# Re-timing the first 46 steps, the exponential's table, the fold blocks and the last group of a fused attention and feed-forward kernel

## The chip, the cores and the metric

The kernel runs on one core of one Trainium2 chip. The metric is the device time in microseconds (us) of one execution. PE is the tensor engine, PEld its weight loads, DVE is VectorE, ACT is ScalarE, POOL is GpSimd and SP is SyncE.

## The reference

Cross-covariance attention on 4 batches of 6080 rows and 256 columns is followed by a feed-forward block on all 24320 rows. The result is float32.

```python
def _attn_ref(q, k, v, tau):
    qn = q / (np.linalg.norm(q, axis=1, keepdims=True) + 1e-06)
    kn = k / (np.linalg.norm(k, axis=1, keepdims=True) + 1e-06)
    s = kn.transpose(0, 2, 1) @ qn / tau
    s = s - s.max(-1, keepdims=True)
    a = np.exp(s)
    a /= a.sum(-1, keepdims=True) + 1e-09
    return (v @ a).astype(np.float32)          # (4, 6080, 256)

def _moe_ref(x, w_in, w_out, s, b):            # x: (24320, 256)
    h = x @ w_in                               # 256 -> 2048
    r = np.maximum(h, 0.0)
    g = s * (r * r) + b
    return (g @ w_out).astype(np.float32)      # 2048 -> 256
```

## The kernel before

The attention matrix of a batch is only 256 x 256, so the kernel never forms `v @ a`. It multiplies the attention matrix into `w_in` ("folds" it) and gets a weight `wa` for each batch. The rows are cut into 48 groups of 512 (the last is shorter), and each group takes 16 steps. A step makes one 128-wide block of h with two 128x512 matmuls. ACT takes the relu of two steps at a time, and the squares are shared between ACT and DVE.

The second matmul of groups 1 to 46 is a scheme of seven products in place of eight. It needs sums S1 to S4 of blocks of g, which DVE makes for each group, and combinations T1, T2, T3 and N4 of blocks of `w_out`, which are made once, early in the program. Groups 0 and 47 use a plain second matmul ("slots" of four 128x256 matmuls). Meanwhile the q and k rows of the next batch arrive in chunks, and PE accumulates their product for the next attention matrix ("gram").

In these traces PE keeps the order in which the loop below emits its instructions, even where it has to stand: in the changed kernel a gram matmul waits 2.00 us for its load, and the h block that is emitted behind it starts only after it, at 76.09 us, though the last relu before it had ended at 74.94. So that order is the schedule. `at_step` puts a piece of side work at the end of a step.

```python
qk_pool = pool("qk_pool", 6)       # q/k chunks, and at first the four pieces of w_out
...
def exps():                        # Gram.finish_ops
    st["e"] = sm_pool.tile([P, CH, C], FP16, tag="eT", name="eT")
    for j in range(CH):
        po(nc.scalar.activation(out=st["e"][:, j, :], in_=st["t"][:, j, :], func=AF.Exp,
                                scale=st["r"][:, 0, j : j + 1]))
...
def fold_both(f0, n):              # first two blocks of w_in, for group 0
    def f():
        wa_ps = h_tile("wa_ps")    # one PSUM tile, read by ACT (m = 0) and DVE (m = 1)
        for m in range(CH):
            fold_mm(f0, n, m, wa_ps[:, m, :n])
        for m in range(CH):
            scaled(f0, n, m, wa_ps[:, m, :n])
    return f
...
w_pieces = []                      # w_out, 4 pieces of 512 KB
for i in range(NPIECE):
    w32 = qk_pool.tile([P, 4, C], FP32, tag="qk", name="w32")
    ...
for i, f in enumerate(fin[9:]):                        # the other fold blocks
    at_step(max(0, i // 2 * 4 - 1) + i % 2, f)
for i in range(NPIECE):
    at_step(6 + i, lambda i=i: cast_w_out(i))          # DVE: fp16 copy for groups 0 and 47
for i in range(NPIECE + 1):
    at_step(10 + i, lambda i=i: rowconst_sum(i))       # DVE: row sums of w_out
at_step(21, rowconst_mm)
for i in range(NPIECE):
    at_step(14 + 2 * i, lambda i=i: combine_w(i))      # DVE: 4 combinations
    at_step(22 + 3 * i, lambda i=i: cast_w(i))         # ACT: T2 and T3, last readers of a piece
...
for b in range(1, B):                                  # q/k chunks of the next batch
    w0 = first_group[b - 1] * FT + (26 if b == 1 else 6)
    for c in range(NCH):
        sc = w0 + span * c * JC / n
        at_step(max(3, sc - 16), lambda gr=gr, c=c: gr.load(c))
        ...
PLAG = {0: 11, NG - 1: 5}
SQUARES = {3: (0, 1, nc.scalar), 5: (1, 2, nc.scalar), 8: (2, 4, nc.vector),
           12: (4, 6, nc.vector)}
SUMS = {2: 1, 3: 2, 6: 3, 10: 4}
for s in range(NS + FT):
    g, m = divmod(s, FT)
    if g < NG:
        mm1(g, m)
    ...                                                # products of the group before
    for gp in plain:
        mp = s - PLAG[gp] - gp * FT
        if 0 <= mp < FT:
            plain_mm2(gp, mp)
    if g < NG and m % 2 == 1:
        relu(g, m // 2)
    ...
    if m == 0 and 0 < g and g - 1 not in plain:
        square(g - 1, 6, 8, nc.vector)
    if 0 < g and g - 1 not in plain and m in SUMS:
        sums_of(g - 1, SUMS[m])
    for f in side.pop(s, []):
        f()
```

## Time and profile before

| kernel | median us | range us | runs |
|---|---|---|---|
| before | 732.67 | 732.56 to 733.0 | 3 |

The busy shares of the page (engine, busy us, share of the span, instructions):

```profile
PE 706.2 (97%) x7618; PEld 510.1 (70%) x7618; DVE 626.5 (86%) x877; ACT 537.5 (74%) x574; POOL 82.3 (11%) x158
```

PE has 24.6 us without work in 730.8, and 14.2 of these lie before 38 us, in the load of the first batch. The list of PE's waits tells whose they are (total us, times, longest). The prediction shows four of its lines; these are the two largest (three more, of 0.5 us or less, are left out):

```profile
PE s_ps L142 <- ACT qk L133: 9.0, 2, 7.1
PE s_ps L142 <- DMA qk<-in_q_dram: 4.6, 6, 1.1
```

Both belong to the load of the first batch, before 38 us. In the timeline (start us, duration us, engine, line, operation, count, and in brackets the idle time just before and what ended it) two places matter. The first is the matmul that reads the first sum of group 1, the second the first gram matmul of chunk 2 of batch 1, at step 40. Neither waits:

```profile
72.90 0.44 PE L683 MATMUL o_ps<-T,S 128*128 128x128 f16 x5
...
76.03 0.38 PE L142 MATMUL s_ps<-qk 128*128 128x256 f16 x2
```

### The profile page before, as it was taken

To read this page: it belongs to the slowest core of one execution; us is meant where nothing else is said; L and a number is where in the kernel's file an instruction comes from. 1 tells how busy PE (TensorE), PEld (TensorE's weight loads), DVE (VectorE), ACT (ScalarE), POOL (GpSimd) and SP (SyncE) were. 2 spreads that over 40 slices of the span, in tenths; PEclk is the share of its full clock that TensorE was granted. 3 is DMA by queue.
4 is the path that set the end of the run, shared out by engine and by line. 5 is a ranking of instruction groups with operands and counts; after the bars stand their busy time and mean duration, and the time that the engine had idled before them with its cause. 6 is when DMAs were issued, how large, how long until landed. Compare 5 with 4: busy or idle time off the path is not lost.

```text
span 730.8 us, 17839 instructions
## 1 busy us (share of the span) xinstructions
PE 706.2 (97%) x7618; PEld 510.1 (70%) x7618; DVE 626.5 (86%) x877; ACT 537.5 (74%) x574; POOL 82.3 (11%) x158
## 2 busy tenths in 40 slices
PE   4788999999999999999999999999999999999997
PEld 3555777776677777776677777777668777777776
DVE  4779999988889989988788989998888888888886
ACT  4468877788777777887777778777877777777772
POOL 4523110001111110001010210000000000000000
PEclk9999999999999999999999999999999999999999
DMA  9999995235487764333666685332333333321201
GB/s 236 209 250 134 205 165 96 58 92 123 92 146 161 121 99 95 91 70 73 131 125 137 121 147 126 70 66 66 83 73 78 87 74 73 97 57 60 65 30 74
DMA packets 81600, 79.57 MB, mean 109 GB/s; under 512 B 55696, under 2 KB 56528, under 8 KB 81520
## 3 DMA queue, kind: packets, MB, share of 16 engines
q0 software_dynamic: 21472, 39.46, 31.8%
q1 hardware_dynamic: 59616, 37.64, 19.9%
q8 instruction: 60, 0.98, 0.6%
q10 hardware_dynamic: 432, 1.31, 0.5%
q14 instruction: 20, 0.16, 0.1%
HBM read 78.91 MB, written 24.90 MB: 142 GB/s over the span
## 4 chain that ended last, share of the span: by engine, by line
PE 85%; ACT 6%; DVE 4%; DMA 4%; issue 1%; POOL 0%; ACTq 0%; POOLq 0%; DVEq 0%
PE h_ps L541 41%; PE o_ps L683 37%; PE s_ps L142 4%; ACT r L551 3%; DMA qk<-in_q_dram 2%; PE wa_ps L274 2%; DMA raw<-in_q_dram 1%; ACT g L562 1%; DVE g L564 1%; PE o_ps L589 1%; ACT L247 1%; ACT sq L165 1%; DVE acc L427 0%; ACT L222 0%; DVE w_out L448 0%
## 5 line engine op out<-in xcount | busy, mean ns | idle before, releaser
L551 ACT ACTIVATE r<-h_ps 128x1024 f16<-128x1024 f32 (+1 forms) x384 | 388.6, 1015 | 162.0 <-PE h_ps L541 158.6
L541 PE MATMUL h_ps<-vT,wa 128*128 128x512 f16 (+7 forms) x1632 | 452.5, 364 | 4.4 <-ACT r L551 3.1
L683 PEld LDWEIGHTS <-S 128*128 128x128 f16 x2944 | 198.1, 98 | 86.6 <-issue 1.3
L683 PEld LDWEIGHTS <-g 128*128 128x128 f16 x2208 | 155.0, 98 | 74.1
L564 DVE TENSOR_TENSOR g<-r 128x2048 f16<-128x2048 f16 (+2 forms) x154 | 176.7, 1148 | 21.7 <-ACT r L551 21.4
L683 PE MATMUL o_ps<-T,S 128*128 128x128 f16 x2208 | 183.6, 219 | 1.1 <-DVE S L609 0.7
L541 PEld LDWEIGHTS <-wa 128*128 128x128 f16 x1632 | 136.5, 98 | 25.7 <-issue 4.8
L683 PE MATMUL o_ps<-w_out,g 128*128 128x128 f16 x1472 | 134.2, 219 | 0.0
L569 DVE SCALAR_TENSOR_TENSOR o_sb<-o_ps,s_out,u 128x256 f32<-128x256 f32 x138 | 66.3, 480 | 51.6 <-PE o_ps L683 49.6
L562 ACT ACTIVATE g<-r 128x1024 f16<-128x1024 f16 x92 | 97.0, 1054 | 0.0
L320 POOL DMA_DIRECT2D v<-in_v_dram x48 | 25.7, 535 | 514.7 <-DMA vT<-v 334.1
L142 PE MATMUL s_ps<-qk 128*128 128x256 f16 (+1 forms) x384 | 70.5, 285 | 13.6 <-ACT qk L133 9.0
L569 DVE SCALAR_TENSOR_TENSOR u<-o_ps,s_out,rowconst 128x256 f32<-128x256 f32 x138 | 65.9, 478 | 2.4 <-PE o_ps L683 2.4
L683 PE MATMUL o_ps<-N,g 128*128 128x128 f16 x736 | 63.5, 219 | 0.0
L683 PE MATMUL o_ps<-w_out,S 128*128 128x128 f16 x736 | 63.4, 219 | 0.0
L165 ACT ACTIVATE sq<-qk 128x1024 f16<-128x1024 f16 (+3 forms) x49 | 50.4, 1033 | 10.1 <-DMA qk<-in_k_dram 4.9
L611 DVE TENSOR_TENSOR S<-S,g 128x2048 f16<-128x2048 f16 x46 | 56.3, 1224 | 1.3
L609 DVE TENSOR_TENSOR S<-g 128x2048 f16<-128x2048 f16 x46 | 55.9, 1214 | 0.0
L615 DVE TENSOR_TENSOR S<-g,S 128x2048 f16<-128x2048 f16 x46 | 55.9, 1214 | 0.0
L613 DVE TENSOR_TENSOR S<-g 128x2048 f16<-128x2048 f16 x46 | 55.8, 1214 | 0.0
L142 PEld LDWEIGHTS <-qk 128*128 128x128 f16 (+1 forms) x384 | 33.2, 102 | 19.6 <-DVE qk L132 8.3
L162 DVE TENSOR_TENSOR sq<-qk 128x1024 f16<-128x1024 f16 (+3 forms) x49 | 33.0, 673 | 2.2 <-DMA qk<-in_q_dram 2.2
(67 smaller groups left out, 280.9 us busy)
## 6 DMA issues: line engine op xcount, KB each, us to landing
out_dram<-o_sb SPq DMA_DIRECT2D x46, 512.0 KB, 3.0
v<-in_v_dram POOLq DMA_DIRECT2D x47, 256.0 KB, 3.8
qk<-in_k_dram POOLq DMA_DIRECT2D x42, 256.0 KB, 6.6
qk<-in_q_dram POOLq DMA_DIRECT2D x42, 256.0 KB, 7.6
vT<-v SPq DMA_TRANSPOSE x182, 2.8
w<-in_moe_w_out_dram POOLq DMA_DIRECT2D x4, 512.0 KB, 11.3
raw<-in_q_dram ACTq DMA_DIRECT2D x2, 512.0 KB, 6.9
raw<-in_k_dram SPq DMA_DIRECT2D x2, 512.0 KB, 6.7
```

Of the source, the lines that this page charges most:

```text
L142: po(nc.tensor.matmul(self.s_ps[:, ch, :], kc[:np_, j, ts(ch, P)], qc[:np_, j, :], start=(c == 0 and j == 0 and ch == 0), stop=(c == len(s ...
L165: po(nc.scalar.activation(out=st["sq"][:np_, 1, js, :], in_=kc[:np_, js, :], func=AF.Square))
L541: po(nc.tensor.matmul(dst, wa[:, ci, ts(m, P)], src, start=(ci == 0), stop=(ci == CH - 1), skip_group_check=True))
L551: po(nc.scalar.activation(out=r16[:, :, i % 2, :n], in_=h_tiles.pop((g, i))[:, :, :n], func=AF.Relu))
L562: po(nc.scalar.activation(out=dst, in_=src, func=AF.Square))
L564: po(nc.vector.tensor_mul(dst, src, src))
L569: po(nc.vector.scalar_tensor_tensor(out=dst, in0=src, scalar=s_out, op0=ALU.mult, in1=add, op1=ALU.add))
L609: po(nc.vector.tensor_add(S[1], A21, A22))
L611: po(nc.vector.tensor_sub(S[2], S[1], A11))
L613: po(nc.vector.tensor_sub(S[3], A11, A21))
L615: po(nc.vector.tensor_sub(S[4], A12, S[2]))
L683: po(nc.tensor.matmul(st[name][:, j, :], a()[:, i, ts(j, P)], w[:, i, :], start=first, stop=last, skip_group_check=True))
```

## The change

Its intent is to keep PE fed where it waits for ACT and DVE. It has five parts.

1. The 16 output slots of group 0 go to steps 11 to 33 instead of 11 to 26, so that the steps after 26 aren't h matmuls alone.
2. The preparation of `w_out` (casts, row sums, combinations, T casts) is spread out to follow the arrival of its pieces. Three casts move from DVE to ACT, and the combinations are ordered so that neighbours don't depend on each other.
3. The exponential's table is loaded by a small activation a few steps ahead (`ready`), and the two exponentials stand in different steps.
4. The two first fold blocks write a PSUM tile for each reader, the factor 1/LAM moves into the summed column, and both folds of the second block come at step 0.
5. In the last group, the first two sums are done in halves and one square goes to ACT.

```diff
+            def ready():
+                po(nc.scalar.activation(out=warm, in_=ones32[:, 0:1], func=AF.Exp))
-            def exps():
-                ... both exponentials ...
+            def exps(j):
+                ... one exponential ...
...
-                                            ones16[:, 0:1], start=(ch == 0 and j == 0),
+                                            parts16, start=(ch == 0 and j == 0),
-                po(nc.vector.tensor_scalar_mul(out=st["rs"], in0=r_ps, scalar1=1.0 / LAM))
-                po(nc.vector.reciprocal(out=st["rs"], in_=st["rs"]))
+                po(nc.vector.reciprocal(out=st["rs"], in_=r_ps))
...
-                    wa_ps = h_tile("wa_ps")
+                    two = [self.bank("wa_ps", CH, C)[:, 0, :n], h_tile("wa_ps")[:, 0, :n]]
...
+    FIN = (0, 3, 3, 6, 8, 10, 13)
-        at_step(max(0, i // 2 * 4 - 1) + i % 2, f)
+        at_step(i // 2 * 4 - 1 + i % 2 if i > 1 else 0, f)
+    RC = (13, 16, 19, 21, 23)      # row sums
+    CO = (7, 14, 18, 24)           # casts of w_out: the first on DVE, the others on ACT
+    CW = (17, 20, 25, 27)          # combinations, for two pieces at a time
+    CT = (32, 34, 36, 38)          # T2 casts; T3 casts six steps later
-        at_step(6 + i, lambda i=i: cast_w_out(i))
+        at_step(CO[i], lambda i=i: cast_w_out(i))
-        at_step(10 + i, lambda i=i: rowconst_sum(i))
-    at_step(21, rowconst_mm)
+        at_step(RC[i], lambda i=i: rowconst_sum(i))
+    at_step(30, rowconst_mm)
-        at_step(14 + 2 * i, lambda i=i: combine_w(i))
-        at_step(22 + 3 * i, lambda i=i: cast_w(i))
+        at_step(CW[i], lambda i=i: combine_w(i // 2, i % 2))
+        at_step(CT[i], lambda i=i: cast_w(T2, i))
+        at_step(CT[i] + 6, lambda i=i: cast_w(T3, i))
-                at_step(8, lambda g=g: transpose_v(g))     # group 1
+                at_step(12, lambda g=g: transpose_v(g))
...
+    LAST = {0: last_squares, 2: lambda: sums_of(NG - 2, 1, NP // 2, NP),
+            3: lambda: sums_of(NG - 2, 2, 0, NP // 2), 5: lambda: sums_of(NG - 2, 2, NP // 2, NP)}
-            mp = s - PLAG[gp] - gp * FT
-            if 0 <= mp < FT:
-                plain_mm2(gp, mp)
+            for mp in range(FT):
+                if s == gp * FT + PLAG[gp] + (mp * 3 // 2 if gp == 0 else mp):
+                    plain_mm2(gp, mp)
```

More of the change, by code (lines that the diff above doesn't have):

```diff
@@ L242, in turn @@
                             st["t"][:, j, ts(ch, P)], st["s"][:, ch, ts(j, P)], ident32))
-            def exps():
-                st["e"] = sm_pool.tile([P, CH, C], FP16, tag="eT", name="eT")
-                for j in range(CH):
-                    po(nc.scalar.activation(
-                        out=st["e"][:, j, :], in_=st["t"][:, j, :], func=AF.Exp,
-                        scale=st["r"][:, 0, j : j + 1]))
-                self.wa = apool.tile([P, CH, Dff], FP16, tag="wa16", name="wa16")
+            def ready():
+                po(nc.scalar.activation(out=warm, in_=ones32[:, 0:1], func=AF.Exp))
+            def exps(j):
+                if j == 0:
+                    st["e"] = sm_pool.tile([P, CH, C], FP16, tag="eT", name="eT")
+                po(nc.scalar.activation(
+                    out=st["e"][:, j, :], in_=st["t"][:, j, :], func=AF.Exp,
+                    scale=st["r"][:, 0, j : j + 1]))
+                if j == 0:
+                    self.wa = apool.tile([P, CH, Dff], FP16, tag="wa16", name="wa16")
             def sums():
@@ L279, in f @@
                 def f():
-                    wa_ps = h_tile("wa_ps")
+                    two = [self.bank("wa_ps", CH, C)[:, 0, :n], h_tile("wa_ps")[:, 0, :n]]
                     for m in range(CH):
-                        fold_mm(f0, n, m, wa_ps[:, m, :n])
+                        fold_mm(f0, n, m, two[m])
                     for m in range(CH):
-                        scaled(f0, n, m, wa_ps[:, m, :n])
+                        scaled(f0, n, m, two[m])
                 return f
@@ L301, in finish_ops @@
                       for m in range(CH)]
-            return [norms, recip, turn, exps, sums] + folds
+            return [norms, recip, ready, turn, lambda: exps(0), lambda: exps(1), sums] + folds
         def bank(self, name, a, b):
@@ L351 @@
     nc.vector.memset(ones16, 1.0)
+    parts16 = consts.tile([P, 1], FP16)
+    nc.vector.memset(parts16, 1.0 / LAM)
     ones32 = consts.tile([P, P], FP32)
@@ L415 @@
     fin[1]()
+    fin[2]()
     keep_busy(5, w_in16[:, 0, :P], w_in16[:, 0, :NW])
-    fin[2]()
+    fin[3]()
     transpose_v(0)
-    for f in fin[3:9]:
+    for f in fin[4:11]:
         f()
@@ L435, in rowconst_mm, with combine_w, cast_w_out, cast_w @@
         po(nc.vector.tensor_scalar_mul(out=rowconst, in0=rc_ps, scalar1=b_bc))
-    def combine_w(i):
-        w = w_pieces[i].rearrange("p (i h) c -> p h i c", h=2)
-        B11, B12 = w[:, 0, :, :P], w[:, 0, :, P:]
-        B21, B22 = w[:, 1, :, :P], w[:, 1, :, P:]
-        part = ts(i, 2)
-        po(nc.vector.tensor_sub(T1[:, part, :], B12, B11))
-        po(nc.vector.tensor_sub(B12, B22, B12))
-        po(nc.vector.tensor_add(B11, B11, B12))
-        po(nc.vector.tensor_sub(N4[:, part, :], B21, B11))
-    def cast_w_out(i):
-        po(nc.vector.tensor_copy(out=w_out16[:, ts(i, 4), :], in_=w_pieces[i]))
-    def cast_w(i):
-        w = w_pieces[i].rearrange("p (i h) c -> p h i c", h=2)
-        po(nc.scalar.copy(out=T2[:, ts(i, 2), :], in_=w[:, 0, :, :P]))
-        po(nc.scalar.copy(out=T3[:, ts(i, 2), :], in_=w[:, 0, :, P:]))
+    def combine_w(i, k):
+        for n in (2 * k, 2 * k + 1):
+            for p in (2 * i, 2 * i + 1):
+                w = w_pieces[p].rearrange("p (i h) c -> p h i c", h=2)
+                B11, B12 = w[:, 0, :, :P], w[:, 0, :, P:]
+                B21, B22 = w[:, 1, :, :P], w[:, 1, :, P:]
+                part = ts(p, 2)
+                if n == 0:
+                    po(nc.vector.tensor_sub(T1[:, part, :], B12, B11))
+                elif n == 1:
+                    po(nc.vector.tensor_sub(B12, B22, B12))
+                elif n == 2:
+                    po(nc.vector.tensor_add(B11, B11, B12))
+                else:
+                    po(nc.vector.tensor_sub(N4[:, part, :], B21, B11))
+    def cast_w_out(i):
+        if i == 0:
+            po(nc.vector.tensor_copy(out=w_out16[:, ts(i, 4), :], in_=w_pieces[i]))
+        else:
+            po(nc.scalar.copy(out=w_out16[:, ts(i, 4), :], in_=w_pieces[i]))
+    def cast_w(T, i):
+        w = w_pieces[i].rearrange("p (i h) c -> p h i c", h=2)
+        po(nc.scalar.copy(out=T[:, ts(i, 2), :], in_=w[:, 0, :, :P] if T is T2 else w[:, 0, :, P:]))
     side = {}
@@ L459, in at_step @@
         side.setdefault(int(s), []).append(f)
+    FIN = (0, 3, 3, 6, 8, 10, 13)
     first_group = [b * N // TG for b in range(B)]
-    for i, f in enumerate(fin[9:]):
-        at_step(max(0, i // 2 * 4 - 1) + i % 2, f)
+    for i, f in enumerate(fin[11:]):
+        at_step(i // 2 * 4 - 1 + i % 2 if i > 1 else 0, f)
     at_step(14, lambda: po(nc.vector.tensor_scalar_mul(
         out=s_out, in0=s_bc, scalar1=1.0 / (LAM * LAM))))
+    RC = (13, 16, 19, 21, 23)
+    CO = (7, 14, 18, 24)
+    CW = (17, 20, 25, 27)
+    CT = (32, 34, 36, 38)
     for i in range(NPIECE):
-        at_step(6 + i, lambda i=i: cast_w_out(i))
+        at_step(CO[i], lambda i=i: cast_w_out(i))
     for i in range(NPIECE + 1):
-        at_step(10 + i, lambda i=i: rowconst_sum(i))
-    at_step(21, rowconst_mm)
+        at_step(RC[i], lambda i=i: rowconst_sum(i))
+    at_step(30, rowconst_mm)
     for i in range(NPIECE):
-        at_step(14 + 2 * i, lambda i=i: combine_w(i))
-        at_step(22 + 3 * i, lambda i=i: cast_w(i))
+        at_step(CW[i], lambda i=i: combine_w(i // 2, i % 2))
+        at_step(CT[i], lambda i=i: cast_w(T2, i))
+        at_step(CT[i] + 6, lambda i=i: cast_w(T3, i))
     for g in range(NG):
@@ L506, in fin_step @@
             for i, f in enumerate(ops):
-                at_step(int(s) + 1 + ((0, 3, 6, 9, 13)[i] if i < 5 else 16 + (i - 5) * 3), f)
+                at_step(int(s) + 1 + (FIN[i] if i < 7 else FIN[6] + 3 + (i - 7) * 3), f)
         at_step(w1 - fin_len, fin_step)
@@ L601, with sums_of @@
     S = {}
-    def sums_of(g, n):
-        G = g_tiles[g]
+    def sums_of(g, n, i0=0, i1=NP):
+        G = g_tiles[g][:, :, i0:i1]
         A11, A12 = G[:, 0, :, : TG // 2], G[:, 1, :, : TG // 2]
         A21, A22 = G[:, 0, :, TG // 2 :], G[:, 1, :, TG // 2 :]
-        S[n] = spool.tile([P, NP, TG // 2], FP16, tag=f"S{n}", name=f"S{n}")
+        if i0 == 0:
+            S[n] = spool.tile([P, NP, TG // 2], FP16, tag=f"S{n}", name=f"S{n}")
+        T = {k: t[:, i0:i1] for k, t in S.items()}
         if n == 1:
-            po(nc.vector.tensor_add(S[1], A21, A22))
+            po(nc.vector.tensor_add(T[1], A21, A22))
         elif n == 2:
-            po(nc.vector.tensor_sub(S[2], S[1], A11))
+            po(nc.vector.tensor_sub(T[2], T[1], A11))
         elif n == 3:
-            po(nc.vector.tensor_sub(S[3], A11, A21))
+            po(nc.vector.tensor_sub(T[3], A11, A21))
         else:
-            po(nc.vector.tensor_sub(S[4], A12, S[2]))
+            po(nc.vector.tensor_sub(T[4], A12, T[2]))
     def seven_items(g):
@@ L697, with last_squares @@
     SUMS = {2: 1, 3: 2, 6: 3, 10: 4}
+    def last_squares():
+        sums_of(NG - 2, 1, 0, NP // 2)
+        square(NG - 2, 7, 8, nc.scalar)
+        square(NG - 2, 6, 7, nc.vector)
+    LAST = {0: last_squares, 2: lambda: sums_of(NG - 2, 1, NP // 2, NP),
+            3: lambda: sums_of(NG - 2, 2, 0, NP // 2), 5: lambda: sums_of(NG - 2, 2, NP // 2, NP)}
     for s in range(NS + FT):
@@ L722 @@
             square(g, *SQUARES[m])
-        if m == 0 and 0 < g and g - 1 not in plain:
+        if g == NG - 1 and m in LAST:
+            LAST[m]()
+        elif m == 0 and 0 < g and g - 1 not in plain:
             square(g - 1, 6, 8, nc.vector)
-        if 0 < g and g - 1 not in plain and m in SUMS:
+        elif 0 < g and g - 1 not in plain and m in SUMS:
             sums_of(g - 1, SUMS[m])
```

## The prediction

> **What bounds the kernel now.** I read four views in this order: the page's busy shares, a table of stretches, the list of what the tensor engine (PE) waited for, and the timeline at each of those waits. The busy shares say 706.2 of 730.8 us for PE, with VectorE (DVE) at 86% and ScalarE (ACT) at 74%. The table of stretches (PE, PEld, DVE, ACT, POOL busy, then clock, DMA share, GB/s) shows where the missing 25 us lie.
>
> ```profile
> 0.00:10.00 10.00, 1.87 (x8) 1.12 (x8) 1.51 (x4) 2.76 (x4) 5.41 (x16) 1.00 0.87 259
> 50.00:60.00 10.00, 10.00 (x70) 6.76 (x69) 9.86 (x18) 5.28 (x6) 0.07 (x1) 1.00 1.21 167
> 60.00:70.00 10.00, 8.17 (x49) 4.62 (x48) 9.01 (x18) 9.67 (x16) 4.16 (x8) 1.00 0.80 132
> 200.00:650.00 450.00, 448.63 (x4978) 327.29 (x4976) 392.84 (x532) 342.29 (x358) 39.23 (x74) 1.00 0.48 99
> 710.00:720.00 10.00, 9.31 (x130) 8.37 (x128) 8.78 (x15) 4.01 (x6) 0.00 (x0) 1.00 0.14 54
> ```
>
> Most of the idle time is the load of the first batch, before 38 us, which the change leaves alone. From 200 to 650 us PE lacks 1.4 us in 450. So only three places can give anything: 38 to 70 us, the batch changes and the last group. PE's own waits name them (total, times, longest):
>
> ```profile
> PE h_ps L541 <- ACT r L551: 3.1, 7, 0.6
> PE h_ps L541 <- DVE wa L269: 1.1, 2, 0.7
> PE o_ps L683 <- DVE S L609: 0.7, 1, 0.7
> PE o_ps L589 <- DVE wa L269: 0.2, 1, 0.2
> ```
>
> Matmul ends are modelled, so a wait of 0.6 in this list costs about 0.16 us more of issue time: two 128x512 matmuls are shown as 0.59 us, yet the next pair starts 0.43 us later. I therefore count losses from start to start.
>
> [...] the load at 336.15 follows a relu that ended at 336.13. [...] the DVE half of a fold block waits for the ACT half. [...] dependent 128x256 subtractions start 0.45 us apart, independent ones 0.34 us apart (61.27 to 61.61).
>
> **The change part by part.** A step is one h block; g is the group of 16 steps.
>
> *A, first fold blocks (38.6 to 39.9 us).*
>
> ```profile
> 38.61 0.16 DVE L261 TENSOR_SCALAR rs<-r_ps 128x2 f32<-128x2 f32 x1
> 38.80 0.17 DVE L262 RECIPROCAL rs<-rs 128x2 f32<-128x2 f32 x1
> 39.46 1.00 DVE L269 TENSOR_SCALAR wa<-wa_ps,rs 128x128 f16<-128x128 f32 x3 [0.49 <-ACT wa L267]
> 39.87 0.38 PE L541 MATMUL h_ps<-vT,wa 128*128 128x512 f16 x1 [0.39 <-DVE wa L269]
> ```
>
> Folding 1/LAM into the summed column removes the first line (0.16 and 0.03 of gap). A tile for each reader lets DVE start beside ACT, which takes off the 0.39 us that PE waits. Against that, the last fold block now needs a third PSUM bank that ACT must read first (about 0.2 us). Estimate: 0.4 us gained. The exponential's table was not on this path: its load ended at 37.20, the transposed scores at 37.41.
>
> *B, steps 0 to 12.*
>
> ```profile
> 43.97 0.39 PE L541 MATMUL h_ps<-vT,wa 128*128 128x512 f16 x1 [0.71 <-DVE wa L269]
> 49.53 0.38 PE L589 MATMUL o_ps<-w_out,g 128*128 128x256 f16 x2 [0.19 <-DVE wa L269]
> ```
>
> The second fold moves from step 1 to step 0, ahead of a square that DVE performs after a relu. Eight pairs of matmuls at 0.43 us should take 3.44 us from 39.87; PE is ready for the next at 44.20, so 0.87 us were lost. The later wait cost 0.36. Together 1.2 us. The transposes moved to step 12 are the same work. A and B: about 1.55 us by step 13.
>
> *C, steps 13 to 40, where the first group's output now fills 24 half-slots.* Before, the output ends at step 26, and until step 35 PE has only the h blocks, faster than ACT empties them:
>
> ```profile
> 61.15 0.59 PE L541 MATMUL h_ps<-vT,wa 128*128 128x512 f16 x2 [0.39 <-ACT r L551]
> 63.62 0.59 PE L541 MATMUL h_ps<-vT,wa 128*128 128x512 f16 x2 [0.57 <-ACT r L551]
> 67.94 1.02 PE L541 MATMUL h_ps<-vT,wa 128*128 128x512 f16 x4 [0.25 <-ACT r L551]
> 69.79 0.59 PE L541 MATMUL h_ps<-vT,wa 128*128 128x512 f16 x2 [0.62 <-ACT r L551]
> ```
>
> From start to start these lose 0.56, 0.74, 0.43 and 0.78, together 2.5 us. Spreading the same 16 slots over steps 11 to 33 removes them as they stand. Three things give part of it back. (1) ACT takes three w_out casts (about 0.94 us apart, as its other 128x1024 casts) at steps 14, 18 and 24. Adding relus (0.93 us from start to start) and two squares, ACT is behind by about 0.3 us at step 24 and 0.6 at step 26. (2) DVE has the row sums and the 16 combinations in steps 13 to 27. Their new order puts independent ones next to each other, 0.34 instead of 0.45 us. I added DVE's work up from step 13: it catches up at step 32, waits for relu 7, then does the square 1.15, gram square 0.6, the output's evacuation 1.41 and the first sum 1.21. The product that reads that sum comes about 0.3 us too early. So 2.5 - 0.9 - 0.3 = 1.3 us are left. (3) The w_out pieces hold four of six q/k buffers. Before, the T3 cast frees them at step 22:
>
> ```profile
> 62.94 0.53 POOL L126 DMA_DIRECT2D qk<-in_k_dram  x1 [2.48 <-ACT T L453]
> 72.19 0.56 POOL L126 DMA_DIRECT2D qk<-in_k_dram  x1
> ```
>
> The first line is the load of chunk 2 of batch 1, used by PE at step 40. Now T3 comes at step 38. The buffer that is free first is then chunk 0's, after its DVE square at step 32; the second line shows such a reuse, 0.6 us after that square (70.92 plus 0.68). By my sum the q load is issued about 4.7 us before PE wants it. Loads in this stage land in 4.7 us on an idle queue (the one after 62.94) and in 7.6 in traffic (65 to 68 us). Estimate: PE waits 1.3 us, between 0 and 3. C then nets about 0, at best 1.3.
>
> *D, batches 1 to 3.*
>
> ```profile
> 336.15 1.28 ACT L247 ACT_TABLE_LOAD   x1
> 337.45 0.84 ACT L247 ACTIVATE eT<-t_ps,rnrm 128x256 f16<-128x256 f32 x2
> 339.25 0.59 PE L541 MATMUL h_ps<-vT,wa 128*128 128x512 f16 x2 [0.42 <-ACT r L551]
> ```
>
> The load and both exponentials are one block of 2.1 us on ACT, just before two squares. At the first batch change PE lost 0.57 and then 0.22 us from this (163.36 to 163.93, 165.57 to 165.79), 0.8 us for each of three batches. The warm-up moves the load to a step without squares, where ACT's relus leave 0.6 us in each 1.64, and the exponentials stand two steps apart. Gain: 0.6 us each, 1.9 together; the square root's load stays.
>
> *E, the last group.* PE lost 0.85 us (714.17 to 715.02) waiting for the first sum, behind a 1.22 us square. Halves of 0.6 us and one square sent to ACT remove that: 0.8 us.
>
> Sum: 0.4 + 1.2 + 0 + 1.9 + 0.8 = 4.3 us, so 732.67 - 4.3 = 728.4.
>
> **The rivals.** *The q/k buffers become the wait.* If chunk 2 must wait for T3 itself (step 38) rather than for chunk 0, the load comes some 4 us later; PE then stands about 5 to 6 us at step 40, and C turns to minus 4: about 732.5. For it: the first line above does wait for that cast. Against: chunk 6 took chunk 0's buffer without any cast. *DVE becomes the bound of 50 to 72 us.* It is 9.86 of 10 us busy there before. If the combinations still take 0.45, that is 16 x 0.11 = 1.8 us more, and the first sum comes 2 us late: about 730. *All of C is real* and the load lands in time: 727. *ACT is overfull at steps 34 to 44*, where seven T casts of 0.3 us now meet two squares and two gram squares: up to 1 us more, though the wait at step 40 would hide it.
>
> **Range and chances.** The four sure parts, A, B, D and E, give 3.5 to 4.7 us; C is between -4 and +1.5. That makes 726.5 to 733, with most weight at 727 to 730. I predict 728.5, range 726.4 to 731.8. Two per cent are 14.7 us: more than all of PE's idle time after the head, so faster has 1%; a loss of that size needs several stalls of the chunk-2 kind, 1%.
>
> **What would show it.** The first h matmul near 39.45 without a wait on DVE; no wait on wa at step 4; the output evacuation of group 0 only after step 33; no waits on relus of 0.4 or more at 60 to 70 us; a table load some 8 us ahead of each later exponential and no wait after it; no wait on S near 714. PE's list should have a new line, s_ps waiting for a q/k load near 75 us, of 0 to 3 us. I am wrong if that line is over 4 us, if S of group 1 is waited for by over 1 us, or if the change in D only moves the wait to the relu after the new load.

The predicted gain came to 0.4 + 1.2 + 0 + 1.9 + 0.8 = 4.3 us. Readings of the trace before: the exponential's table load takes 1.28 us and starts 0.02 us after the relu ahead of it, DVE idles 0.49 us until ACT has scaled its half of the first fold block (39.46), and neighbouring combinations start 0.45 us apart when one needs the other, 0.34 us when not. In part A, the 0.2 us for the last fold block is the author's estimate without a derivation; a 128x128 scaling on ACT is shown with 0.36 us in the trace before.

## The result, and the profile after

| kernel | median us | range us | runs |
|---|---|---|---|
| before | 732.64 | 732.56 to 733.0 | 4 |
| after | 729.75 | 729.59 to 729.99 | 4 |

The ratio is 0.996 (95% interval 0.9943 to 0.9977): a gain of 2.9 us, within 2%. Here and below a ratio is the mean time of one kernel's runs over that of the other's of the same rounds, so not quite the ratio of the medians.

The busy shares after:

```profile
PE 705.5 (97%) x7618; PEld 509.7 (70%) x7618; DVE 623.9 (86%) x873; ACT 541.6 (74%) x582; POOL 82.4 (11%) x158
```

PE has the same 7618 matmuls and is busy 0.7 us less, while the span is 2.9 us shorter. ACT has gained 4 us of work and DVE lost nearly 3: that is mostly the three casts. The list of PE's waits after:

```profile
PE s_ps L142 <- ACT qk L133: 7.0, 1, 7.0
PE s_ps L142 <- DMA qk<-in_q_dram: 6.8, 8, 2.0
PE s_ps L142 <- DVE qk L132: 1.8, 1, 1.8
...
PE h_ps L566 <- ACT r L576: 0.4, 1, 0.4
...
PE o_ps L710 <- DVE S L636: 0.2, 1, 0.2
...
PE o_ps L710 <- ACT T L470: 0.2, 1, 0.2
```

The waits on the relu went from 3.1 us to 0.4, those on `wa` are gone, and the one on S went from 0.7 to 0.2. New is a longest wait of 2.0 us on the load of q, where the longest before was 1.1. The table of stretches says when (PE, PEld, DVE, ACT, POOL busy, clock, DMA share, GB/s):

```profile
50.00:60.00 10.00, 9.47 (x60) 5.66 (x58) 9.17 (x18) 9.96 (x11) 0.53 (x1) 1.00 1.05 154
60.00:70.00 10.00, 10.00 (x77) 6.86 (x75) 8.96 (x16) 8.46 (x11) 1.05 (x2) 1.00 0.21 30
70.00:80.00 10.00, 7.70 (x80) 5.46 (x79) 8.77 (x13) 7.96 (x13) 4.24 (x8) 1.00 1.14 177
200.00:650.00 450.00, 449.60 (x4993) 328.05 (x4991) 394.28 (x532) 344.32 (x362) 38.77 (x74) 1.00 0.49 100
```

Between 60 and 70 us PE is now full (8.17 of 10 before), and between 70 and 80 us it has a hole of 2.3 us. The long middle stretch has gained 1 us, from the batch changes. The timeline of the hole:

```profile
67.28 0.68 DVE L162 TENSOR_TENSOR sq<-qk 128x1024 f16<-128x1024 f16 x1
68.58 0.53 POOL L126 DMA_DIRECT2D qk<-in_k_dram  x1 [8.74 <-PE h_ps L566]
69.10 0.54 POOL L126 DMA_DIRECT2D qk<-in_q_dram  x1
69.31 0.36 SPq L601 DMA_DIRECT2D out_dram<-o_sb  x1
70.47 0.45 PE L710 MATMUL o_ps<-T,S 128*128 128x128 f16 x5 [0.20 <-DVE S L636]
75.88 0.38 PE L142 MATMUL s_ps<-qk 128*128 128x256 f16 x2 [2.00 <-DMA qk<-in_q_dram]
```

The load of chunk 2 is issued 0.62 us after the DVE square of chunk 0 has ended (67.28 + 0.68 = 67.96): it waited for that chunk's buffer. The bracket names an h matmul instead, which reads no q/k buffer, so this reading is an inference: a load that reused chunk 0's buffer in the kernel before was issued just as long after the square, and experiment 1 confirms it. Before, chunk 2's load was issued at 62.94. The store of group 0 follows at 69.31 and lands 6.9 us later, so it moves its data beside the load. PE gets to the first product on S 2.4 us earlier than before (70.47 against 72.90), and to chunk 2 only 0.15 us earlier (75.88 against 76.03).

How the lead of the changed kernel over the one before grows and shrinks, from the start times in both traces:

| event | before us | after us | lead gained since the start |
|---|---|---|---|
| transposed scores of batch 0 | 36.78 | 37.01 | (head: -0.23) |
| h block of step 13 | 50.61 | 49.41 | 1.20 |
| first matmul on S1 of group 1 | 72.90 | 70.47 | 2.43 |
| gram of chunk 2, step 40 | 76.03 | 75.88 | 0.15 |
| h block of step 46 | 81.02 | 81.17 | -0.15 |
| square root's table, batch 1 | 151.05 | 151.20 | -0.15 |
| the same, batch 2 | 326.37 | 325.75 | 0.62 |
| the same, batch 3 | 501.70 | 500.30 | 1.40 |
| first matmul on S1, last group | 715.02 | 711.99 | 3.03 |
| last output matmuls | 725.06 | 722.10 | 2.96 |

By step 46 everything that the first 46 steps had gained is lost again. In this trace the whole gain of 2.9 us comes from the batch changes and the last group.

The other parts in the trace after. The first h matmul starts without a wait, beside the scalings of the other fold blocks, and a single reciprocal is left ahead of it:

```profile
38.84 0.17 DVE L266 RECIPROCAL rs<-r_ps 128x2 f32<-128x2 f32 x1
39.11 0.61 DVE L273 TENSOR_SCALAR wa<-wa_ps,rs 128x128 f16<-128x128 f32 x2
39.74 0.59 PE L566 MATMUL h_ps<-vT,wa 128*128 128x512 f16 x2
```

At the second batch change the table is loaded 3.6 us ahead of the first exponential, and the h matmul after them shows no wait. The load takes 1.28 us; the small activation behind it starts at 331.45 and the next relu at 331.56:

```profile
330.15 1.28 ACT L246 ACT_TABLE_LOAD   x1
333.76 0.47 ACT L251 ACTIVATE eT<-t_ps,rnrm 128x256 f16<-128x256 f32 x1
335.41 0.47 ACT L251 ACTIVATE eT<-t_ps,rnrm 128x256 f16<-128x256 f32 x1
338.07 0.59 PE L566 MATMUL h_ps<-vT,wa 128*128 128x512 f16 x2
```

In the last group the second half of S1 is a 0.68 us instruction, and the product on it follows at once, without a bracket:

```profile
711.79 0.68 DVE L636 TENSOR_TENSOR S<-g 128x1024 f16<-128x1024 f16 x1
711.99 0.61 PE L710 MATMUL o_ps<-T,S 128*128 128x128 f16 x8
```

### The profile page after: what moved, and what is told of

Same layout as the page of the kernel before. It is cut to its first block, busy times and chain, and to the rows that moved or that the text cites. A ratio compares the mean times of both kernels' runs of the same rounds, so it can differ in the third digit from the quotient of the medians.

```text
span 727.9 us, 17843 instructions
## 1 busy us (share of the span) xinstructions
PE 705.5 (97%) x7618; PEld 509.7 (70%) x7618; DVE 623.9 (86%) x873; ACT 541.6 (74%) x582; POOL 82.4 (11%) x158
## 3 DMA queue, kind: packets, MB, share of 16 engines
q0 software_dynamic: 21472, 39.46, 31.9%
## 4 chain that ended last, share of the span: by engine, by line
PE 89%; DMA 5%; ACT 3%; DVE 2%; issue 1%; POOL 0%; ACTq 0%; POOLq 0%; DVEq 0%
PE h_ps L566 43%; PE o_ps L710 38%; PE s_ps L142 4%; DMA qk<-in_q_dram 3%; PE wa_ps L278 2%; ACT r L576 1%; DMA raw<-in_q_dram 1%; PE o_ps L614 1%; ACT g L587 1%; ACT sq L165 0%; ACT L222 0%; DVE f L178 0%; PE t_ps L241 0%; DVE o_sb L594 0%; DVE S L638 0%
## 5 line engine op out<-in xcount | busy, mean ns | idle before, releaser
L638 DVE TENSOR_TENSOR S<-S,g 128x2048 f16<-128x2048 f16 (+1 forms) x47 | 56.4, 1201 | 1.3
L636 DVE TENSOR_TENSOR S<-g 128x2048 f16<-128x2048 f16 (+1 forms) x47 | 56.0, 1192 | 0.0
L640 DVE TENSOR_TENSOR S<-g 128x2048 f16<-128x2048 f16 x46 | 55.8, 1214 | 0.0
```

What stands on the lines that cost most here:

```text
L636: po(nc.vector.tensor_add(T[1], A21, A22))
L638: po(nc.vector.tensor_sub(T[2], T[1], A11))
L640: po(nc.vector.tensor_sub(T[3], A11, A21))
```

## The experiments

**Theory.** The first 46 steps gave nothing because the T casts, now at steps 32 to 44, hold four of the six q/k buffers longer. The load of chunk 2 then waits for chunk 0's buffer and lands 2 us too late. **Rivals.** The hole is traffic, because the store of group 0 is issued beside that load; or DVE and ACT are behind anyway, so that PE's lead would be lost elsewhere; or the parts of the change don't add up as I had summed them.

Twelve kernels ran, five timed rounds each, in three sets, each set on one chip. The kernel before ran in the same rounds, at medians of 732.64, 732.78 and 732.74 us. These differ by 0.14 us at most, so that results of different sets, and the changed kernel's 729.75, are compared directly. All twelve gave correct results.

### 1. Eight q/k buffers

The changed kernel with two more buffers, so that the load of chunk 2 finds a free one.

```diff
-    qk_pool = pool("qk_pool", 6)
+    qk_pool = pool("qk_pool", 8)
```

> The changed kernel with eight instead of six q/k buffers, nothing else. My theory: the 2.2 us that the tensor engine loses at step 40 (2.00 us in its list of waits, s_ps on a q load, 73.71 to 75.88 from start to start) come from the buffer: the load of chunk 2 starts only at 68.58, 0.6 us after the square that empties chunk 0. With a free buffer it starts long before, the wait goes, and the time falls by 2.0 to 2.3 us to about 727.6. Rival, DMA traffic: the load would be late whatever its buffer is, or scalar and vector engine, both full at 70 to 75 us, would stop the tensor engine at nearly the same place: then the time falls by under 0.7 us.

Measured: 727.71 us (727.35 to 727.93), ratio to before 0.9934 (0.992 to 0.9947), 2.0 us better than the change as it was. The load of chunk 2 is issued 8.9 us earlier, and the gram matmul has no bracket:

```profile
59.67 0.54 POOL L126 DMA_DIRECT2D qk<-in_k_dram  x1
...
73.60 0.38 PE L142 MATMUL s_ps<-qk 128*128 128x256 f16 x2
```

So the hole is the buffer, and its removal is worth what the wait was: nothing else was hidden behind it. (The loads of chunks 3 and 4 still wait for buffers here, at 68.48 and 73.89 us after 6.15 and 4.34 us of idle on GpSimd, but PE does not wait for them.)

### 2. The store of group 0 at step 46

The changed kernel with six buffers. Meant to move the store of group 0 away from the late load.

```diff
-                if js[-1] == nj - 1:
+                if js[-1] == nj - 1 and g == 0:
+                    at_step(46, lambda: store(0))
+                elif js[-1] == nj - 1:
                     store(g)
```

> The changed kernel with the store of group 0 issued at step 46 instead of step 33. The store (512 KB, issued 69.31) runs beside the awaited q load (issued 69.10, landed after 6.7 us, where a lone one takes 4.7). If traffic makes the load late, the wait at step 40 falls from 2.0 to about 0.2 us and the time by 1.8 us. If the late start makes it late and traffic adds only part, the wait falls by 0.5 to 1.3 us. If traffic does not matter: no change, within 0.3 us.

Measured: 728.80 us (728.08 to 729.25), ratio 0.9947 (0.9935 to 0.996). The wait shrinks from 2.00 to 1.12 us:

```profile
65.35 5.03 SPq L347 DMA_TRANSPOSE vT<-v  x4
69.37 0.54 POOL L126 DMA_DIRECT2D qk<-in_q_dram  x1
70.48 0.57 SPq L601 DMA_DIRECT2D out_dram<-o_sb  x1
75.27 0.38 PE L142 MATMUL s_ps<-qk 128*128 128x256 f16 x2 [1.12 <-DMA qk<-in_q_dram]
```

But the edit did less than was meant. Step 46 is at about 81 us, and the store was issued at 70.48: a later place in SP's list of instructions only put it behind four DMA transposes that had followed it before (from 69.79 us). So it still runs beside the load, 1.1 us after the load's issue instead of 0.2, and the transposes start 4.4 us earlier than before. With this lighter traffic (a DMA share of 0.90 from 70 to 80 us, against 1.14 in the changed kernel) the load lands in 5.9 us instead of 6.7, and the wait is 0.9 us shorter. So traffic has a part in the wait. How much the store alone has, and what is left of the wait without it, this run doesn't show. Experiment 1 shows that without the late start there is no wait.

### 3. Exponential's table and both exponentials together again, in batches 1 to 3

```diff
-                po(nc.scalar.activation(out=warm, in_=ones32[:, 0:1], func=AF.Exp))
+                if self.b == 0:
+                    po(nc.scalar.activation(out=warm, in_=ones32[:, 0:1], func=AF.Exp))
-    FIN = (0, 3, 3, 6, 8, 10, 13)
+    FIN = (0, 3, 3, 6, 9, 9, 13)
```

> The changed kernel with the table of the exponential loaded again just before the two exponentials, both in one step, in batches 1 to 3. The tensor engine's wait on a relu of 0.4 us comes back at each of the three batch changes; from start to start the chip lost 0.8 us each there before, so the time rises by 2.0 to 2.4 us. If this part gave nothing: no change.

Measured: 733.60 us median, ratio 1.0007 (0.9994 to 1.0019). The five times fall in two clusters: 732.16 and 732.23, and 733.6, 733.79 and 733.87 at a slightly lower mean clock (0.998 against 0.999 and 1.0). Why three runs are 1.6 us longer stays open. The profiled run, of the lower cluster, is 2.5 us longer than the changed kernel, and the waits on the relu are back after the batch changes:

```profile
PE h_ps L567 <- ACT r L577: 1.7, 4, 0.4
```

```profile
164.32 0.59 PE L567 MATMUL h_ps<-vT,wa 128*128 128x512 f16 x2 [0.42 <-ACT r L577]
```

By the lower cluster the part is worth 2.4 us, as expected: the largest single gain of the change.

### 4. Last group with whole sums and squares

```diff
-        if g == NG - 1 and m in LAST:
-            LAST[m]()
-        elif m == 0 and 0 < g and g - 1 not in plain:
+        if m == 0 and 0 < g and g - 1 not in plain:
             square(g - 1, 6, 8, nc.vector)
```

> The changed kernel with the last group's squares and sums whole again, as before. The wait on the first sum near the end comes back (0.69 us in the list of waits, 0.85 from start to start): time up by 0.7 to 0.9 us, to about 730.5. If the halves gave nothing, no change.

Measured: 730.65 us (730.31 to 730.75), ratio 0.997 (0.9958 to 0.9983), 0.9 us more than the changed kernel, as expected. The wait on the sum is back at 0.7:

```profile
PE o_ps L710 <- DVE S L636: 0.9, 2, 0.7
```

### 5. The old preparation of w_out in the changed kernel

The spread slots stay; casts, row sums and combinations return to their old steps and engines, so the q/k buffers come free early again. The transposes of group 1 were left at step 12.

```diff
-    CO, RC, CW, CT and their at_step lines
+    casts at 6 + i on DVE, row sums at 10 + i, combinations at 14 + 2 * i, T casts at 22 + 3 * i
```

> The changed kernel with the preparation of w_out as it was: casts on the vector engine at steps 6 to 9, row sums at 10 to 14, combinations at 14 to 20 in the old order, T casts at 22 to 31. The w_out pieces then free their buffers at steps 22 to 31 and chunk 2 is loaded early. If the later preparation is only a cost through the buffers, the wait at step 40 is gone and the time falls by 1.5 to 2.3 us. If the vector engine needs the new pacing, it falls behind between steps 6 and 20, relus wait for squares (1.65 us once before the change) and the tensor engine for relus at steps 14 to 24: then the time stays within 1 us of the changed kernel or rises.

Measured: 732.38 us (732.19 to 733.09), ratio 0.9999. The expectation missed, for a reason that neither theory had named:

```profile
54.87 0.68 DVE L338 COPY vT<-vT_ps 128x1024 f16<-128x1024 f16 x1
55.61 1.49 PE L552 MATMUL h_ps<-vT,wa 128*128 128x512 f16 x4 [3.09 <-DVE vT L338]
57.75 1.06 PE L552 MATMUL h_ps<-vT,wa 128*128 128x512 f16 x2
60.77 0.59 PE L552 MATMUL h_ps<-vT,wa 128*128 128x512 f16 x2
```

The copy of group 1's transposes, four steps later than before, now queues behind the old heap of casts and row sums on DVE, and the first h block of group 1 waits 3.09 us for it. After that, the same two matmuls take 1.06 us instead of 0.59. The table of stretches gives the granted clock, the third number from the right (a mean over each stretch):

```profile
55.60:57.70 2.10, 2.09 (x8) 1.08 (x9) 2.07 (x6) 0.56 (x1) 0.00 (x0) 0.61 1.50 117
57.70:60.30 2.60, 2.60 (x12) 1.29 (x10) 2.50 (x6) 0.66 (x2) 0.53 (x1) 0.66 0.49 86
60.30:65.00 4.70, 4.54 (x29) 2.85 (x28) 4.43 (x12) 4.70 (x7) 0.18 (x1) 1.00 0.42 58
```

After an idle time of 3.1 us by the list, or 3.3 from start to start, the mean clock is 0.61 and then 0.66 in the two stretches up to 60.30 us, and 1.00 from there. A block of h, or a slot of four output matmuls, takes 0.85 or 0.86 us from start to start between 56.90 and 59.46, and 0.43 or 0.44 after 60.33. By the means, 2.10 x 0.39 + 2.60 x 0.34 = 1.7 us of PE's full rate are lost (an estimate from these two means). In the 2.0 us hole of the changed kernel, and in the 3 us after it, the clock was 1.00. What makes the clock fall, these traces don't show: this run has one such case. So the run mixes two causes and says nothing of the pacing; experiment 8 mends it. It does show that with the old preparation the move of the transposes to step 12 costs this wait.

### 6. The spread of group 0's slots alone, in the kernel before

```diff
-            mp = s - PLAG[gp] - gp * FT
-            if 0 <= mp < FT:
-                plain_mm2(gp, mp)
+            for mp in range(FT):
+                if s == gp * FT + PLAG[gp] + (mp * 3 // 2 if gp == 0 else mp):
+                    plain_mm2(gp, mp)
```

> The kernel before with the first group's output alone spread over steps 11 to 33; the preparation of w_out, the folds, the exponentials and the end stay. My theory: the four waits on relus between 61 and 70 us (2.5 us from start to start) are only there because that stretch has no output matmuls; spreading takes away 1.5 to 2.3 us, the rest goes to the later evacuation and the vector engine: 730.3 to 731.1. Rival: the vector engine, still with the casts, row sums and slow combinations in one heap, holds relus back (it is 9.86 of 10 us busy), and the spread alone gives under 0.7 us: the paced preparation is what makes it pay.

Measured: 734.08 us (734.0 to 734.24), ratio 1.0018 (1.0005 to 1.0032): slower by 1.3 us. The expected gain is not there; the rival was right.

```profile
60.15 1.02 ACT L551 ACTIVATE r<-h_ps 128x1024 f16<-128x1024 f32 x1 [2.53 <-DVE g L564]
61.23 0.59 PE L541 MATMUL h_ps<-vT,wa 128*128 128x512 f16 x2 [1.43 <-ACT r L551]
63.70 0.59 PE L541 MATMUL h_ps<-vT,wa 128*128 128x512 f16 x2 [1.01 <-ACT r L551]
```

With fewer output matmuls at steps 16 to 26, PE runs through the h blocks faster (step 21 starts at 56.32 us, against 57.56 before), while DVE still has its heap of casts, row sums and combinations (9.86 of 10 us busy from 50 to 60). The squares come late, ACT waits 2.53 us for one of them before it can write its next relu, and PE waits 1.43 and 1.01 us for ACT. The waits that the spread was to remove return earlier and larger.

### 7. The fold blocks alone, in the kernel before

Part 4 of the change; the transposes of group 1 stay at step 8.

```diff
-                    wa_ps = h_tile("wa_ps")
+                    two = [self.bank("wa_ps", CH, C)[:, 0, :n], h_tile("wa_ps")[:, 0, :n]]
-        at_step(max(0, i // 2 * 4 - 1) + i % 2, f)
+        at_step(i // 2 * 4 - 1 + i % 2 if i > 1 else 0, f)
     (and 1/LAM in the summed column)
```

> The kernel before with the fold part alone: a tile for each reader, the column of 1/LAM, and both folds of the second block at step 0 (the transposes stay at step 8). By my sum the first h block is 0.4 us earlier and step 4 does not wait (0.87 us), so step 13 comes 1.2 to 1.6 us earlier. If that lasts, the time is 731.1 to 731.5. Rival: the stretch from 50 to 70 us is set by scalar and vector engine, which swallow it: the waits on relus at 61 to 70 us grow by the same amount and the time falls by under 0.5 us.

Measured: 731.75 us (731.63 to 731.79), ratio 0.9986 (0.9973 to 0.9998): 1.0 us gained, a little under the band. The rival was wrong: the waits on relus stay at 3.1 us in all, and the lead of 1.03 us at step 13 (49.58 against 50.61) is still 1.03 at the first product on S1 (71.87 against 72.90). So nothing is taken back later; the lead is smaller than in the changed kernel from the start. One wait on `wa`, at step 11, has stayed:

```profile
48.49 0.38 PE L590 MATMUL o_ps<-w_out,g 128*128 128x256 f16 x2 [0.19 <-DVE wa L268]
```

It costs 0.34 us from start to start. The scaling that it waits for stands behind the old casts of `w_out` on DVE, so the paced preparation removes it, and not the folds; experiments 8 and 9, with the old preparation, have it too. Besides, the fold matmuls at 40.13 us wait 0.22 us for the load of `w_in`.

### 8. The old preparation, with the transposes back at step 8

Experiment 5 mended.

```diff
-                at_step(12, lambda g=g: transpose_v(g))
+                at_step(8, lambda g=g: transpose_v(g))
```

> As the run with the old preparation in the changed kernel, but with the transposes of group 1 at step 8 again. There the copy of the transposed values stood behind the casts and row sums on the vector engine, the tensor engine waited 3.09 us for it and then ran at half rate until 60 us (granted clock 0.83 from 50 to 60 us). If that is the whole loss of that run, this one has no wait for the copy, nor one for a q/k load at step 40, and is 1 to 2 us faster than the changed kernel: about 728. If the old preparation also makes the vector engine late for squares, relus wait for it at steps 14 to 24 and the time is within 1 us of the changed kernel, 729 to 731.

Measured: 730.29 us (730.02 to 730.49), ratio 0.9966 (0.9954 to 0.9979). The wait at step 40 and that on the copy are gone, and the relu waits of experiment 6 are there again (1.43 and 1.01):

```profile
PE h_ps L552 <- ACT r L562: 2.4, 2, 1.4
```

Against the changed kernel, the pacing (with the transposes at step 12) is worth only 0.5 us with six buffers. Experiment 1, with the pacing and eight buffers, is 2.6 us faster. The old preparation with eight buffers was not run, but no wait on a q/k load is left here after 38 us that more buffers could take away.

### 9. Everything but spread and pacing

Experiment 8 with group 0's slots dense again: only folds, exponentials and last group remain.

```diff
-                if s == gp * FT + PLAG[gp] + (mp * 3 // 2 if gp == 0 else mp):
+                if s == gp * FT + PLAG[gp] + mp:
```

> The changed kernel without its first two parts: the output of group 0 dense at steps 11 to 26, the old preparation, transposes of group 1 at step 8. Folds, exponentials and the halves at the end stay. If the parts add up, the folds alone gave 1.0 us, the exponentials 2.4 (the run with them together), the halves 0.9: about 728.4, so 1.3 us FASTER than the whole change, because spread and pacing with six buffers cost more than they give. If the parts do not add (the folds' gain is swallowed when the others are in), it is 729 to 730, as the changed kernel.

Measured: 728.62 us (728.48 to 728.88), ratio 0.9944 (0.9932 to 0.9957), 1.1 us better than the whole change. The sum of the parts measured one by one, 1.0 + 2.4 + 0.9 = 4.3 us, gives 728.4, so these three add up. The relu waits of the kernel before are back, and still it wins:

```profile
PE h_ps L552 <- ACT r L562: 1.8, 4, 0.6
```

So parts 1 and 2 together cost 1.1 us with six buffers. With eight, experiment 1 is 0.9 faster than this kernel, which has no wait on a q/k load after 38 us either. Experiment 8 differs from this one in the spread alone and is 1.7 us slower: a second sign that the spread without the pacing loses time.

### 10. Dense slots with eight buffers

Meant as the clean test of the spread. The last cast had to come at step 22 and the row-sum matmul at 25 for the dense slots to have their data.

```diff
-    qk_pool = pool("qk_pool", 6)
+    qk_pool = pool("qk_pool", 8)
-    CO = (7, 14, 18, 24)
+    CO = (7, 14, 18, 22)
-    at_step(30, rowconst_mm)
+    at_step(25, rowconst_mm)
     (and the dense slots of experiment 9)
```

> The changed kernel with eight q/k buffers and dense output slots (steps 11 to 26; the last w_out cast at 22 and the row-constant matmul at 25, so that they are in time), the rest of the pacing kept. It tells what the spread itself gives when no load is waited for. If the dense slots leave the tensor engine short of work at steps 27 to 34, the waits on relus come back (2.5 us before the change): 729.2 to 730.2, against 727.7 for the spread with eight buffers. If the pacing alone had removed them, 727.5 to 728.

Measured: 729.86 us (729.82 to 730.03), ratio 0.9962 (0.9949 to 0.9974). The time is in the expected band, for another reason than the one expected:

```profile
PE o_ps L614 <- ACT w_out L466: 1.9, 3, 1.3
```

PE mostly waits for the casts on ACT, which the dense slots reach too early. Not a clean test, then. It shows that these paced casts need the spread slots, as experiment 6 showed that the spread slots need the paced preparation.

### 11. The combinations in their old order, with eight buffers

```diff
-        for n in (2 * k, 2 * k + 1):
-            for p in (2 * i, 2 * i + 1):
+        for p in (2 * i, 2 * i + 1):
+            for n in (2 * k, 2 * k + 1):
     (and eight q/k buffers)
```

> Eight buffers, and the 16 combinations in the old order within each call (a piece's two, then the next piece's), at the same steps. Dependent neighbours start 0.45 us apart, independent ones 0.34, so the vector engine needs some 0.9 us more between 54 and 64 us. In the changed kernel it then sits idle for 1.00 us before the square at 66.14, waiting for a relu: if that idle time takes it up, no change within 0.3 us of 727.7. My prediction gave the new order 1.8 us of effect on the rival's side; if that was right the time rises by over 0.7.

Measured: 727.57 us (727.5 to 727.72), ratio 0.9929 (0.9916 to 0.9943): no difference from experiment 1. From start to start every second combination now takes 0.45 us and the others 0.34, where the changed kernel has 0.335 throughout, although each is shown with 0.42: 0.9 us more in all. (In the kernel before it is three of four that take 0.45, so 1.3 us more; that order was not run.) But DVE stands idle for 1.00 us in the changed kernel a little later, before a square at 66.14 us, because it waits for a relu. What the order saves goes into that idle time; in this run's trace it is gone.

### 12. Three of the casts of w_out on GpSimd, with eight buffers

```diff
-            po(nc.scalar.copy(out=w_out16[:, ts(i, 4), :], in_=w_pieces[i]))
+            po(nc.gpsimd.tensor_copy(out=w_out16[:, ts(i, 4), :], in_=w_pieces[i]))
     (and eight q/k buffers)
```

> Eight buffers, and the three w_out casts moved from ScalarE to GpSimd, which is idle from 50 to 59 us. In the changed kernel ScalarE is 9.96 of 10 us busy there and the tensor engine loses 0.3 and 0.56 us (57.31 to 57.60, 58.90 to 59.46). If ScalarE is the reason: 0.6 to 0.9 us faster than 727.7. If a cast on GpSimd slows the vector engine beside it, or takes so long that the output matmuls wait for it, slower.

Measured: 727.42 us median, in two clusters (727.28, 727.3, 727.42 and 728.46, 728.48), ratio 0.9933 (0.992 to 0.9945): not to be told from experiment 1. The profiled run is one of the longer ones. In it, ACT is freed (7.40 us busy from 50 to 60, against 9.96 in the changed kernel), but DVE pays:

```profile
46.23 2.03 DVE L589 TENSOR_TENSOR g<-r 128x1024 f16<-128x1024 f16 x1 [0.22 <-ACT r L576]
46.66 1.05 POOL L466 CAST w_out<-w 128x1024 f16<-128x1024 f32 x1
48.92 0.60 PE L614 MATMUL o_ps<-w_out,g 128*128 128x256 f16 x4 [1.24 <-DVE w_out L464]
```

The square beside the GpSimd cast took 2.03 us instead of 0.69. DVE's own cast came late by as much, and PE waited 1.24 us for it. Two squares beside the next GpSimd cast, at 49.65, took 2.41 us where the changed kernel's took 1.41. The first square started 0.43 us ahead of its cast, and lost 1.34 us beside a cast that is shown with 1.05. Why the squares are longer there the trace does not show, and the spans of GpSimd are rough.

## Why the prediction was right, and where a step was not

The prediction was 728.5 us (range 726.4 to 731.8), and the kernel takes 729.75. The time is in the range and the class is right. Against the 4.3 us of its sum, the traces give -0.23 (head) + 1.43 + (-1.35) + 2.3 + 0.86 = 3.0 us, so nearly all of the distance is C. By its own steps:

- **A and B, folds: right in sum, one term under the wrong head.** 1.43 us by step 13, counted from the transposed scores, against 1.55. By itself in the kernel before it was worth 1.0 (experiment 7): the 0.36 us of the later wait on `wa`, which the prediction counts here, goes only with the paced preparation.
- **C, steps 13 to 40: the mechanism right, a term of the sum mis-sized.** The waits on ACT fell to 0.30 us (at 57.31) and 0.56 (at 58.90) from start to start, together the 0.9 that was allowed. The wait for the first sum was 0.2 in the list and 0.36 from start to start, where 0.3 was expected. Up to that product C had gained 2.43 - 1.20 = 1.23 us, against 1.3 predicted. The place and kind of the new wait were right too: q/k buffer, chunk 0's square, step 40, with the load issued 4.6 us before PE wants it (73.71 - 69.10), where 4.7 was predicted. The mis-sized term is the step "Estimate: PE waits 1.3 us". The load took 6.7 us to land (the median of the 42 q loads of this size in this trace is 7.6), so that the wait was 2.17 us from start to start (73.71 to 75.88), and C nets -1.35 instead of "about 0". Experiment 2 shows that traffic has a part in it: with the transposes moved ahead and the store 0.9 us later relative to the load, the wait is 0.9 us shorter. A small wait on a T3 cast before 80.90 us, 0.3 us from start to start, was not in the sum at all.
- **D, batch changes: right.** 0.77 us for each batch, 2.3 for three, against 1.9; undone, 2.4 (experiment 3, lower cluster). The table loads come 3.6 us ahead of the first exponential and not "some 8 us"; it was enough.
- **E, last group: right.** 0.86 us in the traces and 0.9 by experiment 4, against 0.8.
- **The rivals.** "All of C is real", 727 us, is nearly what eight buffers give: 727.71. "DVE becomes the bound" did not come: S1 was waited for by 0.2 us. Its sum, 16 x 0.11, was too large, as only 12 of the 16 combinations start 0.45 us apart in the kernel before (1.3 us), and experiment 11 shows that 0.9 us of it costs nothing. "ACT is overfull" shows only as the T3 wait, which eight buffers do not hide: 0.15 us in the list of experiment 1 too. Chunk 2 did not wait for T3 itself, though chunk 3's load, issued at 74.00, did wait for a T cast (4.37 us of idle before it on GpSimd, ended by that cast); PE has no wait of that kind in its list beyond the ones named. The prediction treated the spread as the part that removes 2.5 us of waits "as they stand", and the pacing as what takes some of it back. Experiments 6 and 8 show that this reading is wrong although the sum came out nearly right, which is luck to that extent: the spread without the pacing loses 1.3 us, because the waits come from the heap on DVE as much as from ACT.

**What stays open.** What the spread alone would be worth once the preparation is paced and eight buffers are there (experiment 10 was not clean). Why experiments 3 and 12 each fall into two clusters. How much of the late landing is the store of group 0 alone (experiment 2 did not take it away).

**The version to keep** is the change with eight q/k buffers: 727.71 us (727.57 with the combinations in the old order, which is not a difference), 2.0 us under the changed kernel and 4.9 under the one before.

## What to carry to other kernels

When a re-timing moves the last reader of a buffer, look up what is loaded into that buffer next, and for when: here a delay of some casts by 13 to 16 steps cost 2.2 us at a matmul that has nothing to do with them, and two more buffers paid it back. Spreading PE's work paid here only when the work of the engines that feed PE was spread with it: the spread alone lost 1.3 us (1.7 in the changed kernel), and experiment 10, with the pacing and without the spread, is 1.2 us slower than experiment 9, with neither, though that test was not clean. Look in the trace where a moved instruction went: in experiment 2, thirteen steps later in the program were 1.2 us later on the chip. In a bundle, test the parts one by one, because here three parts of the five carried all of the gain and the other two cost 1.1 us until a third thing, the buffers, was changed.
